# An induced-set attention and a parametric-ReLU feed-forward: the prologue's scores stay in PSUM, and its steps get another order

## The chip, the cores and the metric

The kernel runs on one core of one Trainium2 chip. The metric is the time on the device in microseconds, as the median of several runs. Where a profile is shown, it is that of one execution, recorded by the hardware profiler. Engines are named as the profile names them: PE (TensorE) does matrix products and transposes, with its weight loads in a row of their own (PEld); DVE (VectorE), ACT (ScalarE) and POOL (GpSimd) do the rest; SP (SyncE) issues most of the transfers, in one queue in program order.

## The reference

```python
B, N, m, C = (4, 12480, 32, 128)          # x: B x N x C, inducing: m x C
scale = 1.0 / np.sqrt(C)

def mab(q, kv):
    s = scale * (q @ kv.transpose(0, 2, 1))
    s = s - s.max(-1, keepdims=True)
    a = np.exp(s)
    a /= a.sum(-1, keepdims=True) + 1e-09
    return a @ kv
h = mab(I, x)              # 32 inducing points attend to all 12480 rows of a batch
attn = mab(x, h)           # each row attends to the 32 results

h = attn @ w_in                                        # 128 -> 2048
g = np.maximum(h, 0.0) + alpha * np.minimum(h, 0.0)    # alpha: one per hidden unit
out = g @ w_out                                        # 2048 -> 128
```

Inputs and output are f32; the products run in bf16. The first attention needs all of a batch before its result h is there, and the second attention and the feed-forward need h.

## The kernel before

Rows of a batch are cut into super-tiles of 16 x 128 rows (six of them, and a short one of 192 rows). In the prologue of batch 0 they are handled as 8 *pieces*: piece 0 is the first super-tile, piece 1 the short rest, pieces 2 to 5 the next four super-tiles, pieces 6 and 7 the two halves of the last one.

A piece goes through these steps. The letters are those of the string `order` in the code; a number behind the letter is the piece, a number behind the dot is a part of it (for a whole super-tile part 0 has 8 tiles of 128 rows, parts 1 and 2 have 4 each), and the last letter is the engine (a ACT, v DVE, p POOL).

- `k`: cast a part from f32 to bf16 (`a_cast_part`, L346 on ACT, L348 on DVE or POOL). When the last cast of pieces 0 and 2 is done, the loads of piece 5, and of pieces 6 and 7, are issued into the freed buffers (`load_next`).
- `t`, `c`: transpose a part on PE (L363) and copy it from PSUM into xT (L369 on ACT, L371 on DVE).
- `s`: scores of the 32 inducing points against the piece (`a_scores`, L378), 128 x 512 in one PSUM bank.
- `m`: DVE multiplies the scores by -scale, writes them to SBUF (s1) and takes the row minimum in the same pass (`a_least`, L417; L427 joins it with the pieces before).
- `e`: ACT takes the exponential of s1 with that minimum as bias (`a_exp`, L443).
- `u`, `v`: transpose the exponentials on PE (L481) and copy them to SBUF (L487, L489). `f`: the factor between two running minima (L461).
- `h`, `g`: product with the piece's rows (L498) and its addition to the running sum hs (L514, L523).

Then come steps for the whole batch: `ml` (lowest minimum, L392), `ex`, `mg`, `rb`, `mm`, `mf` (factors), `dx`, `dn`, `pd`, `rec` (denominator), `ph`, `hT` (h, transposed, L627). Then `b`, `b2` (second attention's scores for the first 4 and the other 12 tiles of group 0, L684), `bm`, `bs`, `be` (maximum, subtraction and exponential for the first 4), `rx` (maximum for the other 12, L715), `rl` and `rk` (subtraction for tiles 4 to 7, and for tiles 8 to 15, L719), `re` (exponential for tiles 4 to 7, L813), `bt`, `ba` (first 4 tiles turned on PE, L819, and copied, L827), `w`, `hw` (HW, the product of h with w_in, L638, and its copy, L645).

The feed-forward's weights have steps of their own: `lw` issues the loads of w_in (L1073) and w_out (L1075) into the buffers of pieces 3 and 4, `kwp` casts w_in to bf16 on POOL (L1130) and is followed by a transposing transfer of it (winT, L1185), `om` forms 1 - alpha, and `ww` forms W1 = w_out (1 - alpha) (L1014, four parts) and AW = w_out alpha (L1023, four parts) on POOL. W1 is what the second product uses, AW and winT give a 128 x 128 matrix for the linear part of the activation (L1033). `W` and `Z` steps are products of zeros on PE that nothing reads (`warm`, L1000).

From there on the main loop runs over *visits*: a block is 4 tiles, a block has 4 visits, a visit makes four 128 x 512 pieces of the hidden layer (L848), evicts each with a relu on ACT (L861) or DVE (L863), and the visit after it multiplies them by W1 into an accumulator (L874). Tiles 4 to 7 are turned on PE within the first visit (L819 again); tiles 8 to 15 by POOL (L1193) and a transposing transfer (L1196). Batches 1 to 3 run their first attention in between, with their own steps spread over the visits by a planner, which also chooses who evicts what and which PSUM bank is used.

PSUM has 8 banks. In the prologue `ring` hands out banks 0 to 5 in turn; bank 6 is that of `warm`, bank 7 holds the scores of `b2` (the tile `later`). Each engine executes its instructions in program order, and the order in which the prologue's steps are recorded is the string `order`.

Of the kernel before, what the change touches and what calls it, by code (L numbers as in the profile page):

```python
# [13 lines left out]
COPY = mybir.ActivationFunctionType.Copy  # L14
MULT = mybir.AluOpType.mult
# [6 lines left out]
P = 128  # L22
R = 4
ST = 16
# [6 lines left out]
def kernel(  # L31
# [243 lines left out]
    def ring(shape, dtype=f32):  # L275
        return ps_pool.tile(shape, dtype, name="hh", tag=f"k{plan.bank()}")

    small = ring

    def sums():  # L280

        return ps_pool.tile([P, 512], f32, name="bp", tag=f"k{plan.bank()}")
# [88 lines left out]
            nc.vector.tensor_copy(out=dst, in_=ps[:, :n, :])  # L371

    def a_scores(st, pc):
        ps = small([P, 512])
        parts, cols, q = pc.parts, pc.cols, pc.q
        for g in range(R if pc.full else 1):
            t0 = pc.tile + g * q
            nc.tensor.matmul(  # L378
                ps[32 * g : 32 * g + 32, :cols].rearrange("m (j t) -> m j t", j=q),
                IT[:],  # L380
                st.xT[:, t0 : t0 + q, : pc.last],
                start=True,
                stop=True,
            )
        st.s1p[pc.k] = ps

    def own(st, p):

        return not st.b and p >= EARLY
# [22 lines left out]
    def a_least(st, pc):  # L412
        p, ps = pc.k, st.s1p.pop(pc.k)
        parts, cols = pc.parts, pc.cols
        s1 = s1_pool.tile([P, Q * P], f32, name="s1", tag="s1")
        def work():
            nc.vector.tensor_scalar(  # L417
                out=s1[:parts, :cols],
                in0=ps[:parts, :cols],
                scalar1=-scale,  # L420
                scalar2=None,
                op0=MULT,
                op1=MIN,
                accum_out=(st.rm if own(st, p) else st.mx)[:parts, p : p + 1],
            )
# [45 lines left out]
    def a_e1(st, pc):  # L471
        e1 = e1_pool.tile([P, Q, P], bf16, name="e1", tag="e1")
        n = pc.q
        nc.sync.dma_start_transpose(out=e1[:, :n, :], in_=st.e1T.pop(pc.k)[:, : n * P])
        st.e1[pc.k] = e1
# [237 lines left out]
    def b_most(ps, t0, n):  # L713
        m = sm_pool.tile([P, ST], f32, name="smx", tag="smx")
        nc.vector.tensor_reduce(out=m[:, :n], in_=ps[:, t0 : t0 + n, :], axis=AX, op=MAX)  # L715
        return m

    def b_less(ps, t0, n, m, e, a=0):
        nc.vector.tensor_tensor(  # L719
            out=e[:, a : a + n],  # L720
            in0=ps[:, t0 : t0 + n, :],
            in1=m[:, a : a + n].unsqueeze(2).broadcast_to([P, n, M]),
            op=SUB,
        )
# [270 lines left out]

    def warm(zeros, n, cols):

        ps = ps_pool.tile([P, 512], f32, name="bp", tag=f"k{BANKS - 2}")
        for _ in range(n):
            nc.tensor.matmul(ps[:, :cols], zeros[:, :P], zeros[:, :cols], start=True, stop=True)  # L1000

    warm(blank, 2, BT * P)
    itp = ring([C, M], bf16)
    nc.tensor.transpose(itp[:], ind_b[:], ident[:M, :M])
    nc.scalar.copy(out=IT[:], in_=itp[:])


    a2s = {}
# [28 lines left out]

    rep0 = rep_pool.tile([P, ST, R, M], bf16, name="rep", tag="rep")
    w0 = rep0[:, :, 0, :]
    later = ps_pool.tile([P, ST, M], f32, name="bp", tag=f"k{BANKS - 1}")  # L1040

    def first_products():
        b_products(st, 0, 0, BT)
# [2 lines left out]
    def first_most():  # L1046
        kept["bm"] = b_most(kept["b"], 0, BT)

    def rest_most():
        kept["rm"] = b_most(later, BT, ST - BT)  # L1050
        kept["re"] = new_e()

    def rest_less(t0, n):
        b_less(later, t0, n, kept["rm"], kept["re"], t0 - BT)

    def rest_exp(t0, n):
        b_exp_once(kept["re"][:, t0 - BT :], n, w0[:, t0 : t0 + n])
# [32 lines left out]
    def begin(step):  # L1090


        if step == "Z":
            warm(blank, 1, BT * P)
            return
        if step[0] == "W":
            warm(blank_b, int(step[1:]), 2 * P)
            return
        plain = {
            "mg": lambda: a_max(st),  # L1100
            "rb": lambda: kept.update(rb=a_factors_pe(st)),
            "mm": lambda: a_factors_min(st, kept["rb"]),
            "mf": lambda: a_factors_exp(st),
            "ex": lambda: a_worth(st),
            "ml": lambda: a_lowest(st),
            "lz": lambda: a_from_lowest(st),
            "gs": lambda: a_scale(st),
            "lw": load_weights,
            "dx": lambda: a_weigh(st, nc.gpsimd),
            "dn": lambda: a_den_total(st),  # L1110
            "ww": second_weights,
            "pd": lambda: kept.update(pd=a_den_pe(st)),
            "rec": lambda: a_den_rec(st, kept["pd"]),
            "ph": lambda: kept.update(ph=a_sum_pe(st)),
            "hT": lambda: a_sum_div(st, kept["ph"]),
            "b": first_products,
            "bm": first_most,
            "bs": first_less,
            "be": lambda: b_exp_once(kept["be"], BT, w0[:, :BT]),
            "rx": rest_most,  # L1120
            "rl": lambda: rest_less(BT, BT),
            "rk": lambda: rest_less(H, H),
            "re": lambda: rest_exp(BT, BT),
            "bt": lambda: kept.update(bt=b_turn_pe(w0[:, :BT], BT)),
            "ba": lambda: b_turn_copy(st, 0, 0, BT, kept["bt"], False),
            "b2": lambda: b_products(st, 0, BT, ST - BT, later),
            "w": lambda: a_w(st),
            "al": lambda: kept.update(al=alpha_turn()),
            "alc": lambda: nc.vector.tensor_copy(out=alT[:], in_=kept["al"][:]),
            "kwp": lambda: nc.gpsimd.tensor_copy(out=w_in_b[:], in_=kept["w_in"][:]),  # L1130
            "om": lambda: nc.gpsimd.tensor_scalar(
                out=om_al[:], in0=alT[:], scalar1=-1.0, scalar2=1.0, op0=MULT, op1=ADD
            ),
            "hw": lambda: a_w_copy(st),
            "hwv": lambda: a_w_copy(st, False),
        }
# [4 lines left out]
        p, _, part = step[1:].rstrip("avp").partition(".")  # L1141
        pc = first_pieces[int(p)]
        if f in "tc":
            t0, n = cuts[pc.n][int(part)]
            if f == "t":
                kept["t", p, part] = a_turn_pe(st, pc, t0, n)
            else:
                a_turn_copy(st, pc, t0, n, kept.pop(("t", p, part)), act)
        elif f == "k":
            a_cast_part(st, pc, *cuts[pc.n][int(part)], step[-1])  # L1150
            done = first_pieces[int(p)].s
            if pc.full and step == last_cast[done]:
                load_next(done)
        elif f == "u":
            kept["u", p] = a_e1_pe(st, pc)
        elif f == "v":
            a_e1_copy(st, pc, kept.pop(("u", p)), act)
        else:
            {"s": a_scores, "m": a_least, "e": a_exp, "f": a_fac, "h": a_h, "g": a_add}[f](st, pc)
# [5 lines left out]
    }  # L1165
    assert ST == 16 and NX == 8 and short[2] == 2
    order = """
        k0.0v k1.0p k0.1a k0.2a k2.0p Z t0.1 c0.1a t0.0 k2.2p t0.2 al k3.0p t1.0 c0.0v k2.1a
        c0.2v k3.1p Z s0 t2.1 c1.0a t2.0 alc m0 c2.0v t2.2 om c2.1v k4.0p s1 k5.2p m1 e0
        c2.2a k3.2a e1 f1 s2 t3.2 k5.0p m2 c3.2v u0 e2 t3.0 k6.0p u2 c3.0v v0v u1 v2v k4.1a  # L1170
        k6.1p t3.1 t4.1 W2 t4.0 k4.2a c3.1v k7.1p f2 v1v t4.2 c4.1v c4.2v s3 m3 h0 c4.0a
        k5.1a W2 s4 e3 t5.2 g0 m4 h2 h1 g1 t5.1 t5.0 c5.2a W1 t6.0 g2 u3 k7.0p c5.1a c5.0v
        e4 W1 t6.1 s5 t7.1 v3v W1 t7.0 c6.0a c6.1v m5 f3 c7.0v s6 c7.1a m6 W2 s7 u4 e5 m7 u5
        ml v4v e6 lw lz h3 mg ex u6 g3 v5v h4 gs e7 g4 rb dx u7 mm v6a h5 v7a mf dn h6 h7 g5
        g6 g7 pd W5 ph rec hT W4 b b2 kwp bm w bs rx be rl hw W3 bt ww ba re rk
    """
    waiting = [first_pieces[5:6], first_pieces[6:]]
    last_cast = {}
# [238 lines left out]
```

## Time and profile before

| | |
|---|---|
| median of 3 runs | 591.48 us (591.35 to 591.55) |
| profiled execution | 593.02 us, of which its span 591.1 us |
| instructions | 23015 |
| busy over the span | POOL 217.2 us; the other engines are in the prediction's first lines |
| granted TensorE clock | 1.0 in all of the span |
| DMA | 80.56 MB, mean 136 GB/s; HBM read 28.07 MB, written 25.56 MB |

A group of instructions in the profile reads: line, engine, operation, what it writes and reads, shapes, count, then busy time and the mean of one in ns, then the engine's idle time just ahead of the group and who ended it. A line of the timeline reads: start in us from the span's start, length, engine, line, operation, tiles, count of merged instructions, and in brackets the idle time before it and what ended it. In the chain of waits a line is start, length and what set the time then.

### The profile page before, as it was taken

The numbers are of one execution on the slowest core, as the hardware profiler recorded it, in microseconds if no ns is written. First come the engines' busy times: TensorE is split into PE (matmuls) and PEld (weight loads), VectorE is DVE, ScalarE is ACT, GpSimd is POOL, SyncE is SP. The second block draws the span as 40 slices with busy tenths as digits, with TensorE's granted clock in tenths as the row PEclk, the third lists the DMA queues.
The fourth block names the chain that finished last, engine by engine and source line by source line (L and its number), as shares of the span: only waits on it lengthen the run. The fifth ranks groups of instructions, "written<-read, shape, count | busy, mean of one in ns | idle before, by whom it ended". The sixth has DMA issues, their size and how long they took to land.

```text
span 591.1 us, 23015 instructions
## 1 busy us (share of the span) xinstructions
PE 580.7 (98%) x9443; PEld 436.2 (74%) x9443; DVE 534.4 (90%) x974; ACT 536.8 (91%) x1085; POOL 217.2 (37%) x259
## 2 busy tenths in 40 slices
PE   7899999999999999999999999999999999999997
PEld 3577777777777777777777777777777777777776
DVE  5799999988998998999999899999999999999996
ACT  5699999999999999999998999999999998999986
POOL 3575552523325426313226256124034134144110
PEclk9999999999999999999999999999999999999999
DMA  8786799734188899432256999741331331441321
GB/s 334 252 213 169 153 256 217 116 91 74 38 240 185 184 205 222 103 82 70 77 151 176 216 216 221 143 99 38 92 75 54 91 81 48 118 85 58 91 69 48
DMA packets 121964, 80.56 MB, mean 136 GB/s; under 512 B 103761, under 2 KB 105729, under 8 KB 118785
## 3 DMA queue, kind: packets, MB, share of 16 engines
q1 hardware_dynamic: 121632, 78.99, 56.0%
q8 instruction: 74, 1.21, 0.8%
q14 instruction: 34, 0.27, 0.1%
q10 hardware_dynamic: 224, 0.09, 0.1%
HBM read 28.07 MB, written 25.56 MB: 91 GB/s over the span
## 4 chain that ended last, share of the span: by engine, by line
PE 94%; DMA 3%; POOL 1%; DVE 0%; ACT 0%; issue 0%; DVEq 0%; SPq 0%; POOLq 0%
PE bp L874 66%; PE hh L848 22%; DMA xs<-in_x_dram 3%; PE bp L901 2%; PE hh L684 2%; PE hh L498 1%; PE hh L378 1%; POOL xn L348 0%; PE bp L1000 0%; PE hh L638 0%; DVEq L1412 0%; PE hh L607 0%; PE hh L622 0%; PE hh L1033 0%; PE hh L819 0%
## 5 line engine op out<-in xcount | busy, mean ns | idle before, releaser
L861 ACT ACTIVATE gt<-hh 128x512 bf16<-128x512 f32 x854 | 455.2, 606 | 34.3 <-PE hh L848 29.4
L863 DVE TENSOR_SCALAR gt<-hh 128x512 bf16<-128x512 f32 x706 | 453.4, 683 | 24.5 <-PE hh L848 13.2
L874 PE MATMUL bp<-W,gt 128*128 128x128 bf16 x6240 | 417.2, 220 | 0.7 <-DVE gt L863 0.7
L874 PEld LDWEIGHTS <-gt 128*128 128x128 bf16 x6240 | 349.3, 98 | 85.0 <-issue 76.5
L848 PE MATMUL hh<-a,HW 32*128 32x512 bf16 (+2 forms) x1664 | 156.0, 370 | 0.5 <-DVE a L827 0.5
L798 POOL TENSOR_TENSOR rep<-e,rc 128x2048 bf16<-128x2048 f32 (+2 forms) x26 | 84.8, 3265 | 23.0 <-DVE rc L789 22.6
L766 POOL TENSOR_TENSOR e<-e,smx 128x512 f32<-128x512 f32 (+1 forms) x24 | 24.6, 1027 | 154.6 <-ACT gt L861 79.4
L848 PEld LDWEIGHTS <-HW 32*128 32x128 bf16 x1664 | 40.4, 91 | 42.0 <-issue 5.9
L752 POOL TENSOR_TENSOR t<-e 128x256 f32<-128x256 f32 (+1 forms) x24 | 17.2, 718 | 144.1 <-ACT e L728 144.1
L927 ACT COPY ob<-bp 128x512 f32<-128x512 f32 (+1 forms) x63 | 36.9, 586 | 4.6 <-PE bp L874 1.7
L752 POOL TENSOR_TENSOR t<-t 128x128 f32<-128x128 f32 (+3 forms) x100 | 30.5, 305 | 7.8
L331 POOL CAST xn<-xs 128x2048 bf16<-128x2048 f32 x17 | 32.1, 1891 | 1.3 <-DMA xs<-in_x_dram 0.7
L929 DVE COPY ob<-bp 128x512 f32<-128x512 f32 x31 | 21.2, 684 | 5.2 <-PE bp L874 5.2
L417 DVE TENSOR_SCALAR_CACHE_REDUCE s<-hh 128x512 f32<-128x512 f32 (+2 forms) x29 | 17.9, 619 | 2.2 <-PE hh L378 1.9
L901 PEld LDWEIGHTS <-a 32*128 32x128 bf16 x392 | 14.9, 93 | 5.8 <-issue 0.2
L901 PE MATMUL bp<-HA,a 32*128 32x128 bf16 x392 | 19.1, 214 | 0.0
L443 ACT ACTIVATE e1T<-s,rm 128x512 bf16<-128x512 f32 (+1 forms) x25 | 17.9, 718 | 1.1 <-DVE rm L427 1.0
L761 DVE TENSOR_REDUCE smx<-e 128x16 f32<-128x512 f32 (+1 forms) x24 | 15.9, 661 | 0.0
L728 ACT ACTIVATE e<-e 128x512 f32<-128x512 f32 (+1 forms) x24 | 15.0, 624 | 0.0
L742 ACT COPY e<-hh 128x512 f32<-128x512 f32 (+1 forms) x22 | 13.4, 610 | 0.0
L684 PE MATMUL hh<-hT,xT 128*128 128x32 bf16 x372 | 13.0, 176 | 0.0
L523 DVE SCALAR_TENSOR_TENSOR hs<-hs,fac,hh 128x128 f32<-128x128 f32 (+1 forms) x21 | 7.2, 344 | 6.0 <-PE hh L498 5.3
(117 smaller groups left out, 195.2 us busy)
## 6 DMA issues: line engine op xcount, KB each, us to landing
out_dram<-ob SPq DMA_DIRECT2D x97, 256.0 KB, 2.5
xs<-in_x_dram SPq DMA_DIRECT2D x23, 1024.0 KB, 6.4
xs<-in_x_dram SPq DMA_DIRECT2D x2, 512.0 KB, 8.4
w_in_f<-in_moe_w_in_dram SPq DMA_DIRECT2D x1, 1024.0 KB, 9.9
a<-rep SPq DMA_TRANSPOSE x27, 4.7
xs_left<-in_x_dram SPq DMA_DIRECT2D x4, 96.0 KB, 5.8
xT<-xn SPq DMA_TRANSPOSE x18, 6.6
e<-e1T SPq DMA_TRANSPOSE x18, 3.0
```

The costliest lines, as they stand in the source:

```text
L331: nc.gpsimd.tensor_copy(out=st.xn[s][:], in_=xs[:])
L684: nc.tensor.matmul(ps[w, t, :], st.xT[:, tile0[s] + t, w], hTs[b][:], start=True, stop=True)
L752: nc.gpsimd.tensor_tensor(out=t[:, :n], in0=src[:, :n, :w], in1=src[:, :n, w : 2 * w], op=ADD)
L766: nc.gpsimd.tensor_tensor(out=st.e2[s][:, :n], in0=st.e2[s][:, :n], in1=st.m2[s][:, :n].unsqueeze(2).broadcast_to([P, n, M]), op=SUB,)
L798: nc.gpsimd.tensor_tensor(out=st.rep[s][:, ts], in0=st.e2[s][:, ts].unsqueeze(2).broadcast_to([P, n, R, M]), in1=rc[:, ts].unsqueeze(2).un ...
L848: nc.tensor.matmul(hh[:, q * cols + w.start : q * cols + w.stop], HWs[b][rows, v * P : (v + 1) * P], a2[rows, t0 : t0 + nt, :].rearrange(" ...
L861: nc.scalar.activation(out=gt[:, :cols], in_=hh[:, :cols], func=RELU)
L863: nc.vector.tensor_relu(gt[:, :cols], hh[:, :cols])
L874: nc.tensor.matmul(blk.acc[:, t * C : (t + 1) * C], gt[:, (q * nt + t) * P : (q * nt + t + 1) * P], W1[:, k, :], start=(not blk.begun), st ...
L901: nc.tensor.matmul(blk.acc[w, t * C : (t + 1) * C], blk.a2[rows, blk.t0 + t, w], HAs[b][rows, :], start=(not blk.begun and t == 0), stop=F ...
L927: nc.scalar.copy(out=ob[:, :nt], in_=acc)
L929: nc.vector.tensor_copy(out=ob[:, :nt], in_=acc)
```

## The change

It has four parts.

1. The scale is put into the matrix of the inducing points (IT = -scale x inducing, transposed), so scores leave PE already scaled. In batch 0 the minimum is a plain reduction of the PSUM bank, the exponential reads the same bank, and s1 is not written. In the other batches the pass stays as it is, with a factor of 1.0.
2. Batch 0's scores use two banks of their own, 6 and 7, by the piece's number. `warm` takes a bank of the ring, and the tile for `b2` in bank 7 is handed out when `b2` runs.
3. A new form of the step `u`, with the letter d, turns a piece's exponentials by a transposing transfer on SP's queue (`a_e1`, as the other batches do) in place of `u` and `v`. Piece 4 uses it; in the string it stands directly ahead of `lw`.
4. The string `order` is another one.

```diff
+    def score_bank(k):
+        return ps_pool.tile([P, 512], f32, name="s1p", tag=f"k{BANKS - 2 + k % 2}")
...
     def a_scores(st, pc):
-        ps = small([P, 512])
+        ps = small([P, 512]) if st.b else score_bank(pc.k)
...
+        least = (st.rm if own(st, p) else st.mx)[:parts, p : p + 1]
+        s1 = s1_pool.tile([P, Q * P], f32, name="s1", tag="s1") if st.b else ps
         def work():
-            nc.vector.tensor_scalar(
...
-                scalar1=-scale,
...
+            if st.b:
+                nc.vector.tensor_scalar(
...
+                    scalar1=1.0,
...
+            else:
+                nc.vector.tensor_reduce(out=least, in_=ps[:parts, :cols], axis=AX, op=MIN)
...
     def warm(zeros, n, cols):
-        ps = ps_pool.tile([P, 512], f32, name="bp", tag=f"k{BANKS - 2}")
+        ps = ring([P, 512])
...
-    nc.scalar.copy(out=IT[:], in_=itp[:])
+    nc.scalar.activation(out=IT[:], in_=itp[:], func=COPY, scale=-scale)
...
-    later = ps_pool.tile([P, ST, M], f32, name="bp", tag=f"k{BANKS - 1}")
...
+    def rest_products():
+        kept["later"] = ps_pool.tile([P, ST, M], f32, name="bp", tag=f"k{BANKS - 1}")
+        b_products(st, 0, BT, ST - BT, kept["later"])
...
+        elif f == "u" and step[-1] == "d":
+            a_e1(st, pc)
...
     order = """
-        k0.0v k1.0p k0.1a k0.2a k2.0p Z t0.1 c0.1a t0.0 k2.2p t0.2 al k3.0p t1.0 c0.0v k2.1a
-        c0.2v k3.1p Z s0 t2.1 c1.0a t2.0 alc m0 c2.0v t2.2 om c2.1v k4.0p s1 k5.2p m1 e0
-        c2.2a k3.2a e1 f1 s2 t3.2 k5.0p m2 c3.2v u0 e2 t3.0 k6.0p u2 c3.0v v0v u1 v2v k4.1a
-        k6.1p t3.1 t4.1 W2 t4.0 k4.2a c3.1v k7.1p f2 v1v t4.2 c4.1v c4.2v s3 m3 h0 c4.0a
-        k5.1a W2 s4 e3 t5.2 g0 m4 h2 h1 g1 t5.1 t5.0 c5.2a W1 t6.0 g2 u3 k7.0p c5.1a c5.0v
-        e4 W1 t6.1 s5 t7.1 v3v W1 t7.0 c6.0a c6.1v m5 f3 c7.0v s6 c7.1a m6 W2 s7 u4 e5 m7 u5
-        ml v4v e6 lw lz h3 mg ex u6 g3 v5v h4 gs e7 g4 rb dx u7 mm v6a h5 v7a mf dn h6 h7 g5
-        g6 g7 pd W5 ph rec hT W4 b b2 kwp bm w bs rx be rl hw W3 bt ww ba re rk
+        k0.0a k0.2v Z t0.2 k0.1p al c0.2a alc t0.1 c0.1a t0.0 k1.0p k2.0v c0.0a t1.0 k2.2a
+        k2.1p s0 t2.0 t2.2 k3.1p c1.0a k4.0p m0 c2.0v c2.2a s1 e0 t2.1 c2.1v k3.2a m1 e1
+        k3.0v u0 s2 t3.2 t3.0 m2 v0a u1 c3.2v k4.2a c3.0v v1v t3.1 t4.2 e2 k5.2p c4.2v W1
+        t4.0 u2 k5.0p c3.1a c4.0a k4.1v k5.1a v2v t4.1 k6.0p f2 c4.1v s3 h0 s4 t5.2 k6.1p m3
+        f1 g0 t5.1 m4 c5.1v k7.1p h1 W2 t5.0 t6.0 c5.2a k7.0p W2 t6.1 e3 c5.0v g1 e4 c6.0a
+        s5 t7.1 c6.1v u4d lw u3 m5 W1 t7.0 v3v c7.0v s6 h2 h3 c7.1a m6 e5 s7 f3 g2 e6 m7 ml
+        u5 W3 u6 ex lz mg v5v g3 v6v h4 e7 gs h5 om rb u7 g4 mm h6 dx g5 dn v7a kwp W1 h7 mf
+        pd ww g6 g7 W3 ph rec hT W4 b b2 bm bs W3 w rx be bt ba hw rk rl re
     """
```

`a_e1`, which the new form of `u` calls, issues one transposing DMA on SP's queue (L474): `nc.sync.dma_start_transpose(out=e1[:, :n, :], in_=st.e1T.pop(pc.k)[:, : n * P])`.

More of the change, by code (lines that the diff above doesn't have):

```diff
@@ L414, in a_least @@
         parts, cols = pc.parts, pc.cols
-        s1 = s1_pool.tile([P, Q * P], f32, name="s1", tag="s1")
+        least = (st.rm if own(st, p) else st.mx)[:parts, p : p + 1]
+        s1 = s1_pool.tile([P, Q * P], f32, name="s1", tag="s1") if st.b else ps
         def work():
-            nc.vector.tensor_scalar(
-                out=s1[:parts, :cols],
-                in0=ps[:parts, :cols],
-                scalar1=-scale,
[L421 to L425, printed above, removed]
+            if st.b:
+                nc.vector.tensor_scalar(
+                    out=s1[:parts, :cols],
+                    in0=ps[:parts, :cols],
+                    scalar1=1.0,
+                    scalar2=None,
+                    op0=MULT,
+                    op1=MIN,
+                    accum_out=least,
+                )
+            else:
+                nc.vector.tensor_reduce(out=least, in_=ps[:parts, :cols], axis=AX, op=MIN)
             if not own(st, p):
@@ L1047, in first_most @@
         kept["bm"] = b_most(kept["b"], 0, BT)
+    def rest_products():
+        kept["later"] = ps_pool.tile([P, ST, M], f32, name="bp", tag=f"k{BANKS - 1}")
+        b_products(st, 0, BT, ST - BT, kept["later"])
     def rest_most():
-        kept["rm"] = b_most(later, BT, ST - BT)
+        kept["rm"] = b_most(kept["later"], BT, ST - BT)
         kept["re"] = new_e()
     def rest_less(t0, n):
-        b_less(later, t0, n, kept["rm"], kept["re"], t0 - BT)
+        b_less(kept["later"], t0, n, kept["rm"], kept["re"], t0 - BT)
     def rest_exp(t0, n):
@@ L1125, in begin @@
             "ba": lambda: b_turn_copy(st, 0, 0, BT, kept["bt"], False),
-            "b2": lambda: b_products(st, 0, BT, ST - BT, later),
+            "b2": rest_products,
             "w": lambda: a_w(st),
@@ L1140, in begin @@
         f, act = step[0], step[-1] == "a"
-        p, _, part = step[1:].rstrip("avp").partition(".")
+        p, _, part = step[1:].rstrip("avpd").partition(".")
         pc = first_pieces[int(p)]
```

## The prediction

> **What bounds the kernel now.** I read the page first (shares of busy time, costliest groups, DMA), then the chain of waits over the first 60 us, and then the timeline of each engine over the first 45 us, because the change touches the prologue only.
>
> ```profile
> PE 580.7 (98%) x9443; PEld 436.2 (74%) x9443; DVE 534.4 (90%) x974; ACT 536.8 (91%) x1085; POOL 217.2 (37%) x259
> L874 PE MATMUL bp<-W,gt 128*128 128x128 bf16 x6240 | 417.2, 220 | 0.7 <-DVE gt L863 0.7
> xs<-in_x_dram SPq DMA_DIRECT2D x23, 1024.0 KB, 6.4
> ```
>
> PE is busy for 580.7 of 591.1 us, and the second product (L874) is idle ahead of itself for 0.7 us in all of its 6240 instructions. So from the first visit on PE sets the pace, and what the prologue gains or loses reaches the end one to one. A listing of both built programs shows that on every engine the order from the first visit on is the same; batches 1 to 3 only get a factor 1.0 where -scale stood. The question is therefore when the first visits run.
>
> ```profile
> 11.22 9.67 DMA xs<-in_x_dram
> ...
> 20.94 1.19 POOL xn L348 x2
> ...
> 28.82 0.33 PE hh L638 x4
> ...
> 29.59 0.42 PE hh L819 x16
> ...
> 30.03 0.43 DVE a L827
> ...
> 30.51 0.40 PE hh L848 x4
> 30.91 0.34 PE hh L819 x16
> ...
> 32.07 1.05 PE bp L874 x16
> ...
> 42.22 0.33 PE hh L848 x4
> ```
>
> This is the chain, as start, length and work. The prologue hangs on the last half of x, which lands at 20.9; then come its casts, its tail, HW's product (L638) at 28.82, the first turn (L819, copied at L827), and the first visit at 30.51. The first second-product starts at 32.07, and PE goes from one to the next without a gap. I measure the change at this instruction.
>
> **The change part by part. (1) Scores, minimum and exponential.** The scale moves into IT. The minimum becomes a plain reduction on PSUM, no s1 is written, and ACT reads PSUM.
>
> ```profile
> 29.09 0.55 DVE L715 TENSOR_REDUCE smx<-bp 128x12 f32<-128x384 f32 x1
> 20.94 0.08 DVE L417 DVE_READ_ACCUMULATOR s<-hh 128x1 f32 x1
> ```
>
> A PSUM reduction of 384 columns takes 0.55, so one of 512 takes 0.55 to 0.73 (by proportion). Today's pass is one over the same 512 columns on the same engine, so I take the two as equal. What is left is the read, 0.08 for each of 8 pieces, or 0.6 us of DVE time on an engine that isn't full there. I give it 0.1 on the path (0 to 0.6). An exponential from PSUM has no row; the neighbours are 0.72 (exponential from SBUF) and 0.61 (relu from PSUM, L861, 606 ns on the page), and I keep 0.72. The Trainium skill's page Perfetto Trace Analysis, on larger instructions, puts ScalarE's access overhead at about 93 ns on SBUF and 51 ns on PSUM; by it the two exponentials that count below would be 0.08 us shorter in all. No run shown has that form.
>
> **(2) Banks.** Scores alternate between two banks, each kept until its exponential has read it; warm-up products go to the ring and can now wait for a reader. A score product now waits for the exponential of the piece two before it. Walking through the new order with the durations below, the tightest are piece 5 behind e3 and piece 7 behind e5; both lie on the tail of (6), which has time to spare, so 0 (up to 0.3 if ACT is late).
>
> **(3) Piece 4's turn by a transfer, and the weights behind it.** This removes 4 transposes on PE and one DVE copy (0.42). It adds a transposing DMA on SP's queue, and the weights' loads, which ran ahead, now stand behind it. That is the part that decides.
>
> ```profile
> 13.33 0.33 SPq L1073 DMA_DIRECT2D w_in_f<-in_moe_w_in_dram  x1
> 15.47 0.87 SPq L1075 DMA_DIRECT2D w_out_f<-in_moe_w_out_dram  x1
> DMA to landing us min/median/max: 5.7/7.5/11.3
> w_in_f<-in_moe_w_in_dram SPq DMA_DIRECT2D x1, 1024.0 KB, 9.9
> w_out_f<-in_moe_w_out_dram SPq DMA_DIRECT2D x1, 0.5 KB, 11.3
> L474 SPq DMA_TRANSPOSE e<-e1T x18: 1188/1200/1924, 63.1 to 391.4; - x18
> ```
>
> (The line of landings is that of the nine x loads in the first 60 us.) Today w_in is issued at 13.33 and has landed at 23.2, w_out at 26.8. In the new order SP waits for piece 4's exponential e4, issues the transpose (1.20), and only then w_in. So when does e4 end?
>
> ```profile
> 13.13 0.61 PE L363 MATMUL hh<-ident,xn 128*128 128x128 bf16 x8
> ...
> 14.19 1.04 POOL L348 CAST xn<-xs 128x1024 bf16<-128x1024 f32 x1 [0.72 <-DMA xs<-in_x_dram]
> 16.02 1.01 ACT L369 COPY xT<-hh 128x1024 bf16<-128x1024 bf16 x1 [0.49 <-PE hh L363]
> 16.69 2.72 POOL L348 CAST xn<-xs 128x512 bf16<-128x512 f32 x4 [1.46 <-DMA xs<-in_x_dram]
> 18.33 1.05 ACT L369 COPY xT<-hh 128x512 bf16<-128x512 bf16 x2
> 19.27 0.73 ACT L443 ACTIVATE e1T<-s,rm 128x512 bf16<-128x512 f32 x1
> 20.45 0.31 ACT L461 ACTIVATE fac<-rm 128x1 f32<-128x1 f32 x1
> ...
> 37.16 0.62 ACT L346 CAST xn<-xs 128x512 bf16<-128x512 f32 x1
> ```
>
> Loads land 2.5 us apart (POOL starts on pieces 4 and 5 at 14.19 and 16.69). Piece 4's POOL cast ends at 15.23, its eight transposes (0.61) near 15.9, and ACT's copy c4.0a (1.01) runs to about 17.0. Behind it ACT has the cast k5.1a (0.62), two factors (0.31 each), copy c5.2a (0.55), e3 and e4 (0.73 each): 3.25, so e4 ends near 20.25. Bounds: 19.6, if neighbours overlap as the two copies do (1.05 for two); 21.0, if piece 4's minimum on DVE comes late. Then the transpose to 21.5, and w_in lands 6.4 later (the median of 23 such loads in a queue not backed up): 27.9. It would be 27.2 by the shortest landing of the nine, 5.7, and 29.5 if it is held up as the last half of x was (below).
>
> ```profile
> 25.80 1.89 POOL L1130 CAST w_in_b<-w_in_f 128x2048 bf16<-128x2048 f32 x1
> 27.65 4.04 POOL L1014 TENSOR_TENSOR W<-w_out_f,om_al 128x512 bf16<-128x512 f32 x4
> 31.64 4.04 POOL L1023 TENSOR_TENSOR AW<-w_out_f,alT 128x512 bf16<-128x512 f32 x4
> ...
> 35.70 0.83 POOL L1193 COPY rep<-rep 128x768 bf16<-128x768 bf16 x1
> a<-rep SPq DMA_TRANSPOSE x1, 3.1
> ```
>
> POOL's cast (1.89) ends at 29.8, not 27.69, and HW's product goes at 29.85, not 28.82. On PE the first turn now stands behind it: 0.33, turn 0.42, copy 0.43, hand-offs 0.07, so the first visit starts at 31.1: **+0.6**. The warm-up that fills 29.15 to 29.59 today has been moved ahead of the product, which is why 1.03 shrinks to 0.6.
>
> **(4) The rest of the first group.** Today DVE takes the second block's subtraction ahead of the turn's copy, and ACT its exponential at 30.00. The new order is copy, rk (8 tiles), rl (4 tiles), then the exponential, which block 1's turn on PE (L819 at 30.91) and ACT's first relu wait for.
>
> ```profile
> 29.68 0.29 DVE L719 TENSOR_TENSOR e<-bp,smx 128x128 f32<-128x128 f32 x1
> 30.00 0.31 ACT L813 ACTIVATE rep<-e 128x128 bf16<-128x128 f32 x1
> 30.37 0.41 DVE L719 TENSOR_TENSOR e<-bp,smx 128x256 f32<-128x256 f32 x1
> ```
>
> The copy starts 0.48 before the visit, at 30.6; rk follows 0.34 later (30.03 to 30.37), rl at 31.3 to 31.6, the exponential to 31.95, L819 at 32.0. Today it is 30.91, so the loss is now 1.1: this part adds **+0.5** (0.4 to 0.6; 0 if PE or its relus were held elsewhere until then).
>
> **(5) POOL behind the weights.** w_out lands 3.6 behind w_in as today (26.8 against 23.2), at 31.5; the first W1 part is ready at 32.55, and its product is due at 33.2: no loss. W1 and AW (8.0) end at 39.5, the copy at 40.4, and the transfer (3.1) lands at 43.5. The ninth visit needs it at 42.22 + 1.1 = 43.3: **+0.2**. Today the same transfer has 2.5 us of cover (36.55 + 3.1 = 39.65). On SP, winT's transpose and batch 1's first load also move 2.1 later; ACT casts that load from 37.16 on, 38.3 then, so it has 1.0 less of cover than today, and the bounds are 0 and 0.6 for both together.
>
> ```profile
> 36.55 1.24 SPq L1196 DMA_TRANSPOSE a<-rep  x1
> ```
>
> **(6) Casts and turns in new order.** Piece by piece over three engines; the loads are back to back, so earlier free buffers bring nothing. But without the weights behind it x's last half would land 2.5 after 16.7, at 19.2 instead of 20.9. POOL's four casts end at 19.4 (16.69 + 2.72), so its next can start 1.5 earlier than 20.94, and hT comes 1.5 earlier at most, 0.9 if DVE's queue of copies keeps a part. HW's product waits for w_in all the same, so I put 0 on the path; with that wait gone, this 0.9 to 1.5 is the gain. om moves on POOL into the stretch in which POOL now waits for w_in: 0.
>
> Sum: +0.6 + 0.5 + 0.2 = +1.3, and 0.0 to 0.1 back from (1). The profiled execution took 593.02 with a span of 591.1, so its span would be 592.4; against the runs' median of 591.48 this gives **592.8**.
>
> **The rivals. Faster: x's last half sets the end, and the weights come in time.** Place: the load issued at 11.22. For it: it lands 1.7 later than its spacing, with the weights' loads behind it in the queue. If w_in landed by 26.0 (issued by 20.3, with 5.7), HW's product could go at 28.0 and the first visit at 29.25: -1.3. With (4) hidden, its lower bound, that is 590.2; with (4) it is 590.7. Against: e4 can't end before 19.6, so w_in lands at 26.6 at the earliest. Decides from a landing before 26.
>
> **A wash.** w_in at 26.6 to 27.0, HW's product at 28.6 to 29.0: the visit starts 0.7 to 0.3 early, (4) takes 0.5 back, (5) nothing: 591.5. For it: the low ends of (3). Against: the median of 23 landings.
>
> **Slower still: w_in held up as the last half of x was.** For it: that half came 1.7 late, and in the window from 17 to 21 us one packet of the instruction queue ran among the loads.
>
> ```profile
> q8 instruction: 1, 0.02, 1.7%
> ```
>
> The Trainium skill's page Runtime: NRT & Kernel Launch, on instruction fetch, has blocks of 16 KiB fetched by the sequencer's own DMA queue, at a cost mostly hidden; the row's 0.02 MB is such a block, and whether it held up the load no row here decides. Price: 1.6 more at HW's product, all of it on the path: 594.4. Against: the median of 6.4 was taken under such fetches too.
>
> **That the change doesn't do what it says** (its reads of PSUM stall PE for a bank) would show in the scores alone, and cost a few tenths within the ranges above.
>
> **How the numbers follow.** Forecast 0.52, its own range 592.0 to 593.8 by the bounds of (3) to (5). Held up 0.20, wash 0.11, faster 0.17. The range 590.0 to 594.8 takes in all four, and leaves out further delays and more than the whole gain of x's last half. A change of 0.2% is 1.18 us, about what a measurement of this kernel can tell from none. The forecast's case lies above 592.66 for 0.33 of its 0.52; with the held-up case slower is 0.53. Faster: 0.15 of the 0.17. Same: the 0.19 left of the forecast, the wash, 0.02: 0.32.
>
> **What would show it.** Right: SP issues w_in near 21.5, POOL waits for it until about 27.9, PE waits for the cast ahead of HW's product, L819's second turn waits for ACT, the first second-product stands near 33.2. Wrong: w_in lands before 26, or HW's product waits for hT; a turn that waits for neither; the first second-product at 32.07 or earlier; any difference that grows after 45 us.

## The result and the profile after

| | median | lowest to highest | ratio to before |
|---|---|---|---|
| before | 591.51 us (6 runs) | 591.3 to 591.91 | |
| after | 595.75 us (6 runs) | 594.0 to 596.83 | 1.007, 95% interval 1.0059 to 1.008 |

The change costs 4.2 us, three times the 1.3 forecast, and the time lies above the range. Three things make the difference: the execution that the sum was measured against ran 1.8 us late, the waits for the weights reach further than the sum had them, and the clock of PE was left out of it.

The chain of waits of the changed kernel over its first 60 us (start, length, what set the time; profiled execution of 594.82 us, span 592.1, clock 1.0):

```profile
19.01 0.85 ACT e1T L450 x3
...
20.35 0.85 SPq L481
21.38 5.03 DMA w_in_f<-in_moe_w_in_dram
26.46 1.90 POOL w_in_b L1140
28.38 2.92 SPq L1197
31.35 7.83 DMA xs<-in_x_dram
...
39.73 0.51 ACT gt L868
```

Before, this chain was x's last half, its casts and PE. Now it goes from piece 4's exponential through SP's queue to the load of w_in, POOL's cast of it, the issue of winT's transpose, and the load of batch 1's first rows, whose casts hold ACT and with it the relus. A second path ends within 0.1 us of this one: W1 and AW on POOL behind w_out, then the transfer of tiles 8 to 15 (`a<-rep`, issued at 40.30, landed at 43.6), which the ninth visit needs; that visit stands at 43.68. Line numbers are up to 12 higher than before.

The timeline of the changed kernel, SP's queue, then POOL, then PE (start, length, engine, line, operation; in brackets the idle time ahead and what ended it):

```profile
19.89 1.31 SPq L481 DMA_TRANSPOSE e<-e1T  x1
21.38 0.45 SPq L1083 DMA_DIRECT2D w_in_f<-in_moe_w_in_dram  x1
22.05 0.88 SPq L1085 DMA_DIRECT2D w_out_f<-in_moe_w_out_dram  x1
28.38 2.92 SPq L1197 DMA_TRANSPOSE winT<-w_in_b  x1
31.35 0.58 SPq L322 DMA_DIRECT2D xs<-in_x_dram  x1
```

```profile
26.46 1.89 POOL L1140 CAST w_in_b<-w_in_f 128x2048 bf16<-128x2048 f32 x1 [2.04 <-DMA w_in_f<-in_moe_w_in_dram]
31.41 4.03 POOL L1021 TENSOR_TENSOR W<-w_out_f,om_al 128x512 bf16<-128x512 f32 x4 [3.05 <-DMA w_out_f<-in_moe_w_out_dram]
```

```profile
28.41 0.40 PE L645 MATMUL hh<-w_in_b,hT 128*32 128x512 bf16 x4 [0.91 <-POOL w_in_b L1140]
...
29.55 0.40 PE L855 MATMUL hh<-a,HW 32*128 32x512 bf16 x4 [0.53 <-DVE a L834]
30.43 0.41 PE L826 MATMUL hh<-ident,rep 128*32 128x128 bf16 x16 [0.47 <-ACT rep L820]
...
32.50 1.05 PE L881 MATMUL bp<-W,gt 128*128 128x128 bf16 x16 [0.84 <-POOL W L1021]
```

The reader is to see five waits that the profile of before doesn't have. POOL waits 2.04 for w_in and 3.05 for w_out, so PE waits for POOL's cast ahead of HW's product (L645) and for W1 ahead of the first second-product (L881). The fifth, PE's wait for ACT's exponential ahead of the second turn (L826), is the prediction's part (4).

What the DMA engines do meanwhile stands in the DMA view of the first 40 us, one digit a microsecond (tenths of the 16 engines' time), first the kernel before as profiled, then the changed one:

```profile
DMA  0338999999999999999989995000099959710299
```

```profile
DMA  0349999999999999992006769899959994984000
```

The changed kernel's DMA engines stand empty from 19 to 21 us, with x's last packets through and the weights still held on SP's queue behind e4's transfer; the weights then fill 21 to 31. The kernel before carries x and the weights in one go up to 25 us.

### The profile page after: what moved, and what is told of

It reads as the page before. It is cut to its first block, busy times and chain, and to the rows that moved or that the text cites. A ratio compares the mean times of both kernels' runs of the same rounds, so it can differ in the third digit from the quotient of the medians.

```text
span 592.1 us, 22991 instructions
## 1 busy us (share of the span) xinstructions
PE 579.7 (98%) x9436; PEld 436.0 (74%) x9436; DVE 534.6 (90%) x966; ACT 537.1 (91%) x1085; POOL 216.2 (37%) x258
## 4 chain that ended last, share of the span: by engine, by line
PE 92%; DMA 4%; SPq 1%; ACT 1%; DVE 1%; issue 0%; POOL 0%; DVEq 0%; ACTq 0%
PE bp L881 65%; PE hh L855 21%; DMA xs<-in_x_dram 3%; PE bp L908 2%; PE hh L691 2%; PE hh L505 1%; DMA w_in_f<-in_moe_w_in_dram 1%; PE hh L381 1%; SPq L1197 0%; ACT gt L868 0%; POOL w_in_b L1140 0%; SPq L322 0%; ACT xn L349 0%; DVEq L1424 0%; PE hh L645 0%
## 5 line engine op out<-in xcount | busy, mean ns | idle before, releaser
L881 PE MATMUL bp<-W,gt 128*128 128x128 bf16 x6240 | 417.2, 220 | 1.5 <-POOL W L1021 0.8
L881 PEld LDWEIGHTS <-gt 128*128 128x128 bf16 x6240 | 349.5, 98 | 85.7 <-issue 77.3
L908 PE MATMUL bp<-HA,a 32*128 32x128 bf16 x392 | 19.1, 214 | 0.0
L422 DVE TENSOR_SCALAR_CACHE_REDUCE s<-hh 128x512 f32<-128x512 f32 (+1 forms) x21 | 13.3, 636 | 1.1 <-PE hh L381 1.1
L450 ACT ACTIVATE e1T<-s,rm 128x512 bf16<-128x512 f32 x18 | 13.4, 742 | 0.0
L691 PEld LDWEIGHTS <-xT 128*128 128x128 bf16 x384 | 12.1, 96 | 0.2
```

Of the source, the lines that this page charges most:

```text
L691: nc.tensor.matmul(ps[w, t, :], st.xT[:, tile0[s] + t, w], hTs[b][:], start=True, stop=True)
L881: nc.tensor.matmul(blk.acc[:, t * C : (t + 1) * C], gt[:, (q * nt + t) * P : (q * nt + t + 1) * P], W1[:, k, :], start=(not blk.begun), st ...
L908: nc.tensor.matmul(blk.acc[w, t * C : (t + 1) * C], blk.a2[rows, blk.t0 + t, w], HAs[b][rows, :], start=(not blk.begun and t == 0), stop=F ...
```

## The experiments

Times are medians; "clock" is the mean granted TensorE clock of an execution. The kernel before ran alongside in every batch, at 591.35 to 591.62. No kernel leaves out a part of the computation; r7, r10 and r11 add or drop products of zeros that nothing reads.

### r1_before and r2_after: both kernels again

No edit.

> The kernel before, unchanged, to see the span and the granted clock of each of its executions. Theory A (the new order leaves PE thinly used between 27 and 33 us, and in some executions its clock is then cut, so the median rises by more than the 1.0 us that the profiled span shows): clock 1.000 in nearly all executions of this kernel, spans within 0.5 us of each other, median near 591.5. Theory B (the clock is cut as often in both kernels, and the difference lies outside the span): spans of this kernel spread by 2 us and clocks down to 0.99 too.

> The changed kernel, unchanged, on the same chip. Theory A: spans from 592.1 upward, each 0.5 x (1 - clock) x 594 longer than 592.1, median 594 to 596; if the profiled execution has a clock under 0.998, the slices of the clock show a cut between 27 and 45 us. Theory B: as for the kernel before, spans and clocks alike in both.

Measured: r1_before 591.56 (11 runs, spans 589.4 to 590.2, clock 0.998 to 1.0); r2_after 595.34 (5 runs, 1.0066, 1.0054 to 1.0078, spans 592.8 to 594.8, clock 0.989 to 0.994). Theory A holds in the main. This puts the cost at 3.8 us where the table above has 4.2: three of its six executions of after spent 2.7 us outside their span, the other three and these five 1.8, and the median spans agree (593.4 and 593.5).

The repeated before shows what was wrong with my base. Its timeline, SP's queue, then PE:

```profile
13.00 0.33 SPq L1073 DMA_DIRECT2D w_in_f<-in_moe_w_in_dram  x1
...
25.93 1.44 SPq L1185 DMA_TRANSPOSE winT<-w_in_b  x1
27.49 1.23 SPq L319 DMA_DIRECT2D xs<-in_x_dram  x1
```

```profile
26.97 0.40 PE L638 MATMUL hh<-w_in_b,hT 128*32 128x512 bf16 x4
...
28.72 0.40 PE L848 MATMUL hh<-a,HW 32*128 32x512 bf16 x4 [0.53 <-DVE a L827]
29.05 0.41 PE L819 MATMUL hh<-ident,rep 128*32 128x128 bf16 x16
...
30.27 1.07 PE L874 MATMUL bp<-W,gt 128*128 128x128 bf16 x16
```

And its chain of waits at x's last half:

```profile
10.86 8.24 DMA xs<-in_x_dram
19.15 1.19 POOL xn L348 x2
```

On record that load landed at 20.9 and the first second-product stood at 32.07. Here it lands at 19.1 and the product stands at 30.27: 1.8 earlier, and 1.7 of it is left at the end of the span (589.4 against 591.1). Of the 1.8, 0.4 stood already at the load's issue (10.86 against 11.22) and 1.4 is its landing (8.24 against 9.67). The 28 executions of before in this batch have spans of 589.1 to 590.4; the one on record, 591.1, is outside them. Of the 87 that ran beside all the experiments, one other is that long (591.7). So the profiled execution that the whole sum was measured against was one in which x's last half was held up.

The repeated run of the changed kernel shows the clock. Stretches of it: length, busy us of PE, PEld, DVE, ACT, POOL (with counts), then the granted clock, DMA share and GB/s:

```profile
8.00:12.00 4.00, 1.91 (x25) 1.21 (x23) 2.86 (x8) 3.26 (x8) 1.58 (x2) 1.00 1.02 422
12.00:16.00 4.00, 4.00 (x40) 3.31 (x41) 3.22 (x9) 3.06 (x8) 1.21 (x2) 0.57 0.99 411
...
28.00:32.00 4.00, 2.22 (x60) 1.35 (x60) 2.32 (x7) 2.15 (x5) 0.93 (x2) 1.00 0.99 178
32.00:36.00 4.00, 3.14 (x32) 2.53 (x29) 1.73 (x4) 2.34 (x6) 4.00 (x5) 0.57 0.94 282
```

Twice a stretch in which PE is about half busy is followed by one at a clock of 0.57. Over 4 us that is 3.4 us at half speed (4 x 0.43 x 2); in windows of half a microsecond the clock reads 0.50 from 12.5 to 15.5 and from 33.0 to 35.5. In its timeline the first second-product lasts 1.87 instead of 1.05:

```profile
32.89 1.87 PE L881 MATMUL bp<-W,gt 128*128 128x128 bf16 x16 [0.86 <-POOL W L1021]
```

The profiled execution of after had no such cut; of its 11 executions (both sets) two have a clock of 0.999 or more and spans of 592.1 and 592.2, the other nine 0.989 to 0.996 and 592.8 to 595.0. What a cut costs depends on where it falls: at a clock of 0.994 the spans run from 592.8 to 594.1, where the expectation's estimate gives 593.9 for all of them.

### r3_weights_first: the weights ahead of the transfer

```diff
-        s5 t7.1 c6.1v u4d lw u3 m5
+        s5 t7.1 c6.1v lw u4d u3 m5
```

> The changed kernel with the weights' loads issued ahead of piece 4's transposing transfer instead of behind it. Theory C (the late weights are the main loss: POOL's wait for w_in 2.0 us, for w_out 3.1 us, and the transfers behind them): w_in lands by 23, no wait of POOL for weights, the first visit near 28.6 and the first second-product near 31.1, so a span of 590.0 to 590.8, and with PE busy again no cut of the clock: median 589.5 to 591. If the clock is cut for another reason (fewer products ahead of 15 us), the spans still spread by 2 us. Rival (the scores in PSUM or the order of casts cost it): span within 0.5 of 592.1, median still above 594.

Measured: 597.06 (1.0097, 1.008 to 1.0113), clock 0.985 to 0.994: slower still, far outside theory C's range. SP's queue in it:

```profile
13.04 0.33 SPq L1083 DMA_DIRECT2D w_in_f<-in_moe_w_in_dram  x1
16.24 0.87 SPq L1085 DMA_DIRECT2D w_out_f<-in_moe_w_out_dram  x1
19.76 3.72 SPq L481 DMA_TRANSPOSE e<-e1T  x1
```

The weights are early again, but now the transposing transfer stands behind 2 MB of plain loads: its issue takes 3.72 instead of 1.31 and it lands at 26.89, when w_out does (26.47). Piece 4's product waits for it, and HW's product goes at 32.56. A transfer on this queue waits or makes wait, whichever goes first.

### r4_rl_first: the exponential's subtraction first

```diff
-        ... rx be bt ba hw rk rl re
+        ... rx be rl bt ba hw re rk
```

> The changed kernel with the second block's subtraction and exponential back ahead of the first block's copy (rl before bt, re before rk). By the sum's part (4) the second turn on PE starts 0.3 to 0.5 earlier (30.43 in the changed kernel), but the first second-product still waits for W1, so the span changes by 0 to -0.3. Theory A: the median stays above 594, since PE still waits for the weights.

Measured: 594.44 (594.22 to 597.04; 1.006, 1.0045 to 1.0076). Not told apart from r2_after: its executions have clocks from 0.988 to 1.0, and those without a cut have spans of 592.4, no less than after's 592.1 and 592.2. The first second-product waits for W1 in either order, so what (4) costs is hidden behind that wait here. r6 below shows it without. In the profile the weights are issued 0.5 earlier than in that of after (20.86), and the first second-product goes 0.4 earlier (32.08); yet the ninth visit stands where after has it, for it waits for the transfer behind W1 and AW:

```profile
43.62 0.40 PE L855 MATMUL hh<-a,HW 32*128 32x512 bf16 x4 [0.50 <-DMA a<-rep]
```

### r5_piece4_on_pe and r6_piece4_on_pe_rl: piece 4 back on PE

```diff
-        s5 t7.1 c6.1v u4d lw u3 m5 W1 t7.0 v3v c7.0v
+        s5 t7.1 c6.1v u4 lw u3 m5 W1 t7.0 v3v v4v c7.0v
```

r6 has r4's edit too.

> The changed kernel with piece 4's exponentials turned on PE and copied by DVE as before, so nothing on SP's queue stands ahead of the weights. Theory D (the transposing transfer is the main cause, by way of the queue: behind it the weights come late, ahead of it it waits for them): w_in lands near 23 and w_out near 26.5, no wait of POOL for either, first visit near 28.7, second turn 0.5 late by rl, first second-product near 30.8 against 30.3 in the undisturbed execution of the kernel before; span 589.7 to 590.3, median 591.4 to 592.3. Theory E (the clock of PE is cut because the new order has fewer products between 8 and 15 us): it's still cut there, spans spread up to 592, median 592.5 or more.

> As the run before, with rl ahead of the first block's copy and re ahead of rk too. Theory D: another 0.3 to 0.5 off, first second-product near 30.3, median 590.9 to 591.8, no worse than the kernel before. Theory E: 592 or more.

Measured: r5 591.76 (1.0006, 0.9997 to 1.0015), r6 591.21 (0.9998, 0.9989 to 1.0007). In r5's timeline SP issues the load at 13.06, POOL casts w_in and forms W1 without a wait, and the clock is 1.0 in ten executions of eleven:

```profile
24.86 1.89 POOL L1140 CAST w_in_b<-w_in_f 128x2048 bf16<-128x2048 f32 x1
26.71 4.03 POOL L1021 TENSOR_TENSOR W<-w_out_f,om_al 128x512 bf16<-128x512 f32 x4
```

```profile
30.21 0.41 PE L826 MATMUL hh<-ident,rep 128*32 128x128 bf16 x16 [0.47 <-ACT rep L820]
```

Both times are within theory D's ranges. So 3.6 of the 3.8 us between the kernels go with the one step `u4d`. With the weights in time, the order of `rl` is worth 0.55 by the medians (591.76 to 591.21), against the 0.5 of step (4), and PE's wait of 0.47 for ACT, which r6 doesn't have, fits it. The two kernels' runs overlap, so the size is rough; in the two profiles the first second-product differs by 0.76 (31.38 and 30.62).

### r7_fillers: warm-up products in the thin stretches

```diff
-        ... c0.1a t0.0 k1.0p ... e0 t2.1 c2.1v ... v1v t3.1 t4.2 ... b b2 bm bs W3 w rx be bt ba
+        ... c0.1a t0.0 Z k1.0p ... e0 t2.1 W5 c2.1v ... v1v t3.1 W5 t4.2 ... b b2 bm bs W9 w rx be bt W4 ba
```

> The changed kernel, with products of zeros added where PE waits: one Z ahead of piece 0's scores, five of W ahead of piece 0's turn and five ahead of t4.2, six more ahead of HW's product, four ahead of the first visit. No other step is moved. Theory F (about half of the loss is PE's clock, cut to half in stretches of 3.4 us after stretches in which PE did little): clock 0.998 or more in most executions, spans 592.0 to 592.8, median 593.7 to 594.4 against 595.3 without the fillers. Rival (the clock is cut for another reason, or cuts cost nothing since PE waits anyway): clocks and median as without them, 595 and more.

Measured: 593.39 (1.0035, 1.0022 to 1.0047), clock 0.998 to 0.999 in all five: 2.0 us less than r2_after and below the range expected, though HW's product goes 0.9 later (29.35) than in the profile of after. The first second-product comes at the same instant, now without a wait for W1 ahead of it:

```profile
32.54 1.07 PE L881 MATMUL bp<-W,gt 128*128 128x128 bf16 x16
```

Its spans, 591.0 to 592.7, are partly below the 592.1 of an after without a cut. After's median span is 593.5, 1.4 above the 592.1 without a cut, so about 1.4 of the 2.0 at most is the clock. In its profile the weights are issued 0.65 earlier than in that of after (20.73), batch 1's first load lands 5.6 after its issue, not 7.83, and the visits come 0.9 earlier from there on; its chain runs through W1, AW and the transfer `a<-rep`, which lands at 42.71, just ahead of the ninth visit at 42.75.

### r8_psum_scores_only: parts 1 and 2 alone

The changed kernel with the string `order` of before.

```diff
-        k0.0a k0.2v Z t0.2 k0.1p al ...
+        k0.0v k1.0p k0.1a k0.2a k2.0p Z ...
```

> The kernel before with only the first two parts of the change: scaled IT, plain minimum and exponential on PSUM, two banks for the scores, warm-up products in the ring; step order and piece 4's turn as before. Part (1) and (2) of the sum: -0.1, with 0 to 0.6 for the accumulator reads and up to +0.3 for the banks, so a median of 591.0 to 591.9. Rival (reads of PSUM make PE wait for banks): 592 or more, with PE waiting for ACT ahead of scores.

Measured: 592.01 (1.0011, 1.0002 to 1.0019), just above the range expected. No gain; 0.1% is lost. Grouped by line and shape over the first 40 us (count, busy us, mean ns, idle time ahead), first the changed kernel, then the repeated before:

```profile
L450 ACT ACTIVATE e1T<-s1p,rm 128x512 bf16<-128x512 f32 x5 | 3.4, 689 | 0.0
...
L432 DVE TENSOR_REDUCE mx<-s1p 128x1 f32<-128x512 f32 x3 | 2.1, 689 | 0.1
```

```profile
L443 ACT ACTIVATE e1T<-s,rm 128x512 bf16<-128x512 f32 x5 | 3.6, 724 | 1.0 <-DVE rm L427 0.9
L417 DVE TENSOR_SCALAR_CACHE_REDUCE s<-hh 128x512 f32<-128x512 f32 x5 | 3.4, 687 | 0.9 <-PE hh L378 0.8
```

The reduction takes what the pass took (689 against 687 ns), as step (1) assumed; the exponential is 35 ns shorter from PSUM, 0.07 us for the two that step (1) counts. The rival's sign is there in small: the scores of pieces 2 and 7 now wait for an exponential, as step (2) said of piece 7, and the first visit goes 0.2 later than in the repeated before (28.93). In the changed kernel's order the scores have no such wait. PE's waits up to 32 us in r8:

```profile
PE s1p L381 <- ACT e1T L450: 0.9, 2, 0.5
```

### r9_transfer_only: the transfer alone in the kernel before

```diff
-        ... m6 W2 s7 u4 e5 m7 u5 ml v4v e6 lw lz
+        ... m6 W2 s7 u4d e5 m7 u5 ml e6 lw lz
```

(The code for the form d goes in with it.)

> The kernel before, in its own step order and with its own scores, with one edit: piece 4's turn goes by the transfer (issued on SP's queue ahead of the weights) instead of by PE. Theory A (the transfer ahead of the weights is what costs, whatever the order): e4 ends at 19.5 in the kernel before, so w_in is issued near 20.8 instead of 13.0 and lands near 25.9, POOL's cast ends near 27.8 instead of 25.9 and waits for the load, HW's product goes 1.0 later, W1 1.3 to 2 later and batch 1's first load 2 later: 593 to 595, ratio 1.003 to 1.006, with a granted clock under 0.998 in most executions if PE's idle stretch draws a cut. Theory B (the loss belongs to the new order's thin stretches of PE, the transfer matters only in it): 591.3 to 592.2, clock 0.998 to 1.0.

Measured: 595.72 (1.0068, 1.0056 to 1.0081). One step of the change, put into the kernel before, costs all that the whole change costs, more than either theory had. Its SP queue and POOL:

```profile
20.20 1.31 SPq L474 DMA_TRANSPOSE e<-e1T  x1
21.63 0.51 SPq L1073 DMA_DIRECT2D w_in_f<-in_moe_w_in_dram  x1
...
28.79 2.94 SPq L1187 DMA_TRANSPOSE winT<-w_in_b  x1
31.78 0.58 SPq L319 DMA_DIRECT2D xs<-in_x_dram  x1
```

```profile
31.83 4.04 POOL L1014 TENSOR_TENSOR W<-w_out_f,om_al 128x512 bf16<-128x512 f32 x4 [3.07 <-DMA w_out_f<-in_moe_w_out_dram]
```

The pattern is that of the changed kernel within 0.45 us. The five executions have spans of 593.1 (clock 1.0), 593.4 (0.999) and 593.9 to 594.2 (0.993 to 0.994), against a median of 589.8 for before: 3.3 to 3.6 go without a cut, and the executions with one are 0.5 to 1.1 longer. Why the waits cost 1 us more here than in the changed kernel (592.1 without a cut) isn't settled.

### r10_no_fillers: the kernel before without warm-up products

```diff
-        k0.0v k1.0p k0.1a k0.2a k2.0p Z t0.1 ... g6 g7 pd W5 ph rec hT W4 b b2 ... hw W3 bt ww
+        k0.0v k1.0p k0.1a k0.2a k2.0p t0.1 ... g6 g7 pd ph rec hT b b2 ... hw bt ww
```

> The kernel before with its warm-up products in the order of the prologue taken out (Z and W steps; they write nothing that is read), nothing else. Theory of the clock (thin stretches of PE draw half-speed stretches of 3.4 us): granted clock under 0.998 in most executions, time 593 to 596, ratio above 1.003, though PE waits no longer for any other engine. If the clock has nothing to do with it: PE only loses work that nobody reads, clock 0.998 to 1.0, time 591.0 to 591.7.

Measured: 594.83 (1.0052, 1.0039 to 1.0065), clock 0.990 to 0.994 in all five executions. The stretches:

```profile
4.00:8.00 4.00, 2.34 (x22) 1.25 (x20) 1.13 (x2) 2.18 (x5) 0.42 (x1) 0.98 1.00 395
8.00:12.00 4.00, 3.63 (x27) 1.99 (x25) 2.63 (x9) 2.38 (x6) 2.38 (x3) 0.59 1.02 424
...
24.00:28.00 4.00, 2.37 (x68) 1.58 (x60) 3.24 (x13) 1.01 (x4) 3.27 (x4) 1.00 0.33 73
28.00:32.00 4.00, 3.47 (x66) 2.28 (x59) 3.31 (x7) 3.09 (x7) 4.00 (x5) 0.54 1.10 271
32.00:36.00 4.00, 4.00 (x42) 2.94 (x41) 1.65 (x3) 2.32 (x6) 3.63 (x6) 0.60 0.29 115
```

The weights are early in it, and in its timeline HW's product and the first visit stand within 0.1 of the repeated before (the visit at 28.78). Still 3.2 us are lost, for thin stretches of PE alone draw the cuts: 2.34 and 2.37 busy of 4.00 (the repeated before has 3.80 and 3.63 there), and a clock of 0.54 to 0.60 behind each. This shows the clock as a cause by itself.

### r11_piece4_rl_fillers and r12_order_only: is there a better one?

r11 is r6 with r7's first three warm-up steps. r12 is the kernel before, scores through s1, with r6's string `order`.

> r6_piece4_on_pe_rl (the changed kernel with piece 4 on PE and the exponential's subtraction first) with three warm-up steps more in the thin stretch of PE from 8 to 16 us: Z after t0.0, W5 after t2.1, W5 after t3.1. Theory of the clock: r6's executions have clocks of 0.994 to 1.0, so 591.21 still holds some cuts; with PE filled all executions show 0.998 or more and the time is 590.3 to 591.0, below both kernels. If r6's spread is not the clock's, or if the warm-up products delay the scores: 591.2 to 591.8.

> The kernel before with its own scores (through s1 in SBUF), and with the step order of r6_piece4_on_pe_rl: the new order, but piece 4 on PE and the exponential's subtraction first. If the scores on PSUM are the small loss that r8_psum_scores_only hints at (592.01), the order without them is 590.4 to 591.0, below both kernels. If the new order needs the two banks and the shorter minimum pass: 591.5 to 592.5. If neither counts: 591.0 to 591.6, no different from before.

Measured: r11 591.89 (1.0005, 0.9996 to 1.0014), r12 591.28 (0.9995, 0.9987 to 1.0004). Neither beats the kernel before, nor does r6. In r11 all clocks are 0.998 or more and the time isn't below r6's, so the spread of r6 wasn't the clock's to win. r12 against r6 (591.28 and 591.21) shows the scores on PSUM at nothing in this order; r8's 0.1% belongs to the order of before.

## Why the prediction was wrong, point by point

The instants by which the prediction argued, with the forecast's own base, and what the repeated before and the profile of after (no cut) show:

| | forecast: before, after | measured: before again, after |
|---|---|---|
| HW's product | 28.82, 29.85 | 26.97, 28.41 |
| first visit | 30.51, 31.1 | 28.72, 29.55 |
| second turn | 30.91, 32.0 | 29.05, 30.43 |
| first second-product | 32.07, 33.2 | 30.27, 32.50 |
| ninth visit | 42.22, 43.5 | 40.36, 43.68 |
| span | 591.1, 592.4 | 589.4, 592.1 |

(The forecast's instants are those of the chain; the measured ones are from the timeline, which puts HW's product, the second turn and the ninth visit of before 0.07 earlier.)

**The step that failed is "I measure the change at this instruction", 32.07.** That instant belongs to one execution whose last half of x came late; the weights, issued anew behind the transfer, don't depend on x's last half, so their arrival had to be set against an undisturbed 30.27. The prediction saw the sign of it: it noted that x's last half landed 1.7 late, and made a rival of its coming early ("faster", 590.2). But that gain was already in the median of 591.48: the prediction had this median beside the profiled execution's 593.02, worked the change out against the slower execution and added it to the median. The working that gave 33.2 and +0.2 behind it, set against 30.27, would have been +3.1, or 594.6. That this is near the 595.3 of r2_after is partly luck, since its instants at HW's product and the first visit were 1.4 and 1.6 too late and it holds no cut of the clock. The experiment bears the step out: r6, in which the weights have landed long before 26 and `rl` goes first, meets that rival's condition and takes 591.21, not 590.2.

The rival called a wash shows the same step. Its condition, w_in landing at 26.6 to 27.0 and HW's product at 28.6 to 29.0, was more than met (26.41 and 28.41), and its price was 591.5. Measured from 30.51 the first visit at 29.55 is a gain of 1.0; measured from 28.72 it is a loss of 0.8. The signs of being right came too, the waits named and an issue at 21.38, with the first second-product nearer to 32.07 than to 33.2. The mechanism was seen; the price was taken from the wrong instant.

**(3) was right in mechanism; its landing was not.** w_in was issued at 21.38 (21.5 forecast). It landed 5.0 later instead of the 6.4 of the median, and below the 5.7 taken as the shortest, the DMA engines having stood empty from 19 to 21; so POOL's cast ended at 28.35 instead of 29.8. Priced against the right base it is +0.8 at the first visit (+0.6 forecast).

**(4) was right, 0.5 forecast and 0.55 measured** (r5 to r6, roughly), but in the changed kernel it lies behind W1's wait.

**(5) was mis-sized.** "No loss" at W1 compared a W1 at 32.55 with a product due at 33.2. W1 came when forecast, for w_in landed 1.5 earlier and w_out 4.9 behind it instead of 3.6. The product was due earlier, at some 31.7 by the rest of the chain (32.50 less the wait of 0.84), so W1 became the bound: +2.2 at the first second-product. The "+0.2" for the ninth visit failed by the same step: its transfer landed at 43.6, as forecast (43.5), but the visit was due at 40.36 and not at 42.22. In r4, r7 and r9 the chain of waits runs through that transfer. On SP's queue, winT's issue takes 2.92 instead of 1.44 while w_out's load is still running (r9: 2.94), batch 1's first load goes 3.9 later than in the repeated before (31.35 against 27.49), and ACT's casts of it hold the relus: between the first visit's relus and those at 41 us the lag grows to 3.3. In the profile of after both paths come to that 3.3 at the ninth visit, and 2.7 are left at the end of the span. No run takes one of the two paths away alone.

**The clock was not among the rivals.** PE idle in the prologue was costed as a delay alone. Of 11 executions of after nine have cuts; the median of all 11 spans is 593.5, 1.4 above the 592.1 without. With 592.1 against a median of 589.8 for before, that gives 2.3 for waits and 1.4 for cuts, 3.7 of the 3.8 us between r1_before and r2_after. The split is rough: r7 holds the clock and takes 2.0 off, part of it by weights that come earlier. The Trainium skill's page TensorE: Matmul & The Clock Gate, Part 1, describes a gate that halves the clock by PE's activity in free-running windows of 3.4 us, so that it varies from run to run; the 0.57 over four us in r2_after and the executions of one kernel at 0.989 to 1.0 agree. Which thin stretch draws a cut isn't settled: from 8 to 12 us PE is busy for 2.33 in r5's profile and for 1.94 in r6's, and the clock of both is 1.0 all the same.

**(1), (2) and (6)** were put at nothing or 0.1, and r8, r12 and r6 leave them within 0.1%. That a part of (6), x's last half landing at 19.2, was foreseen and came (19.3) is no gain, since it lands at 19.1 in the undisturbed before.

## What to carry to other kernels

A transfer that replaces a transpose on PE is paid for in the queue that it enters: ask what is queued behind its wait, and what is ahead of it if it is moved. Compare the span of a profile with several other executions before building a sum on it; a late load in it looks like a bound that the change can remove. And where PE runs thin before its dense part, price the idle twice, once as delay and once as a chance of a slower clock behind it; products that nobody reads can be worth their time there.

## What the runs showed of the hardware

Removing nothing but warm-up products made a kernel 0.5% slower (r10_no_fillers). A transposing DMA's issue on SP's queue took 1.31 with the queue empty and 3.72 behind 2 MB of plain loads (r3), and winT's 1.44, or 2.92 while w_out's load ran. Why x's last half came 1.8 late in the profiled execution of before is open: one packet of instructions ran among the loads between 18 and 19 us, but the repeated before has one in the same microsecond, and there the load landed at 19.1. So the packet alone doesn't explain it.
